# Holding the output tiles of a fused attention and gated-unit kernel back: w_out loaded late, a tile every other step, 25 tiles in a block behind the loop

## Chip, cores, metric

One core of a Trainium2 chip. The metric is device time in microseconds (us), the median of a few executions; lower is better. "Span" is the length of the one profiled execution, from which all readings of engines come. A ratio to the kernel before is of runs taken in turns on the same chip; of the experiments, a_noload, a_osb8 and a_bias_odd shared a session with the changed kernel (after_again), the others are compared with it across sessions. A run more than 1.5% above the fastest of its kernel is called slow; fast runs are compared with fast ones.

## The reference, cut to what matters

```python
# q, k, v: [8 batches, 8 heads, 576, 64]
scores = scale * q @ k.T                                   # heads 0-3: sliding window of 32 keys ("plain")
                                                           # heads 4-7: 32 keys, every 4th ("dilated")
x   = softmax(where(mask, scores, -1e9)) @ v               # -> x: [8, 576, 512]
gate = sigmoid(causal_conv(x, conv_w))                     # 5 taps, per channel
out = (gate * (x @ w_val)) @ w_out                         # [8, 576, 512], w_*: [512, 512]
```

## The kernel before

32 steps, one for each pair of heads: four steps a batch, the first two plain, the last two dilated. A step computes scores, exponential, mask and attention product of its pair, normalizes it (xn), and convolves an earlier pair (in the loop, the last but one). A batch that is complete puts eight value products (`vals`) in a list. Their results `y` put output tiles (`outs`, 128 rows x 512 columns, four 512-column products and one eviction each, that is ScalarE's copy of the result out of PSUM, the memory that TensorE writes) in another, and the steps take from both lists. Steps 0 to 7 follow a hand-written program; I call them and what precedes them the **head**, steps 8 or 9 to 31 the **loop**, what follows the start of the first convolution behind the loop (that of pair 30) the **end**.

```python
    def trans_rest(g):                  # last 64 rows of q and k: two transposes, then VectorE's copies
        ...
            nc.vector.tensor_copy(t["kT"][:, :, RM:S], ...)
            for z in range(2):
                nc.vector.tensor_copy(t["qT"][:, z, :, TM:T], ...)
    def make_bias_d():                  # mask of the dilated pairs: GpSimd, and one VectorE minimum
        ...
            nc.gpsimd.affine_select(out=mb, ...)
        nc.vector.tensor_tensor(out=mb, in0=mb, in1=same..., op=ALU.min)
    program = [ "J J T A J J", ... "C M N X V V A T O", "C M N X O K A Q R J J" ]   # O: output tile, J: filler
    ...
    setup_conv_w()
    make_conv_diag(0)
    make_conv_diag(1)
    ...
    next_pair(-1)                       # transposes of pair 0, the rest included
    for i in range(NP):
        ...                             # loads of later groups
        if i == 0:
            make_bias_d()
            prep_v(0)                   # v of pair 0 to bf16, on GpSimd: one cast
        ...
        scores(i, 0); scores(i, 1)
        if i < EARLY: early_rest(i); continue
        if i == ACT_V: upper_v(i)       # ACT_V = 8: two v casts on ScalarE
        run_conv(i - 1); apply_mask(i, 0); after_x(i - 1)
        ...                             # transposes of the next group
        apply_mask(i, 1)
        if c == 0 and outs: run_out()
        elif vals: run_val()
        attn_v(i, 0); attn_v(i, 1); normalize(i)
        ...
        for _ in range((2 if len(outs) > 2 else 1) - (c == 0 and i > NCH)):
            if outs: run_out()
        if vals: run_val()
    ...                                 # two convolutions, 8 value products, 8 tiles
```

The softmax here doesn't subtract the row's maximum and nothing guards it: scores larger than these inputs give would overflow.

## Time and profile before

| | before |
|---|---|
| median of the first three runs | 179.99 us |
| span | 178.5 us |
| first product of step 9's convolution | 56.07 us |
| ... of the first convolution behind the loop | 160.44 us |
| tiles in steps 0 to 7, 8 to 31, behind the loop | 2, 26, 8 |

I use the starts of the convolutions as marks: one a step, all on TensorE. They cut the span into head (56.07), loop (104.37) and end (18.06); step 8's tile lies ahead of the first mark, so by the marks the tiles are 3, 25 and 8. For brevity "the last convolution" below is that first one behind the loop.

### The profile page before, as it was taken

What the parts mean: (1) busy time and instruction counts of PE and PEld (TensorE: products, weight loads), DVE (VectorE), ACT (ScalarE), POOL (GpSimd) and SP (SyncE); (2) the same over time, 40 slices, a digit from 0 to 9 for tenths busy, and PEclk for the clock granted to TensorE, in tenths of its full rate; (3) what the DMA queues carried; (4) which work ended last, traced back from release to release, by engine and by line L of the source; (5) the groups of instructions that cost most, each with busy time, mean ns of one, the idle gap of its engine ahead of it and who ended that gap; (6) DMA issues with size and microseconds to landing.
All of it is one profiled execution on the core that took longest, in us unless ns stands there. A gap on an engine that the chain in (4) does not pass through costs nothing.

```text
span 178.5 us, 7036 instructions
## 1 busy us (share of the span) xinstructions
PE 162.0 (91%) x2925; PEld 107.6 (60%) x2925; DVE 126.0 (71%) x315; ACT 116.9 (66%) x217; POOL 95.8 (54%) x162
## 2 busy tenths in 40 slices
PE   6889888789859999999999999999999999999990
PEld 1445545556447656667766676677667766665540
DVE  5755643996767897779778877987697969773320
ACT  3256556646887776777876788677967796564441
POOL 6633457979663999976089718681998000000000
PEclk9999999999999999999999999999999999999998
DMA  4998999999999999999998999999997222224355
GB/s 150 238 260 269 302 220 231 356 344 212 276 321 252 307 338 309 214 313 305 273 214 257 313 305 254 301 320 299 278 338 223 59 62 62 61 62 109 99 164 162
DMA packets 48731, 42.09 MB, mean 236 GB/s; under 512 B 6853, under 2 KB 43061, under 8 KB 48698
## 3 DMA queue, kind: packets, MB, share of 16 engines
q1 hardware_dynamic: 48144, 41.49, 85.8%
q8 instruction: 23, 0.38, 0.9%
q10 hardware_dynamic: 554, 0.14, 0.4%
q14 instruction: 10, 0.08, 0.2%
HBM read 32.18 MB, written 9.44 MB: 233 GB/s over the span
## 4 chain that ended last, share of the span: by engine, by line
PE 71%; DMA 10%; DVE 7%; SPq 5%; ACT 3%; issue 1%; ACTq 0%
PE ps_bank L703 18%; PE ps_bank L686 15%; PE ps_bank L661 11%; PE ps_bank L408 5%; DMA q_nat<-in_q_dram 5%; PE ps_sc L566 4%; PE ps_sc L580 3%; PE ps_sc L513 3%; DMA vPst<-in_v_dram 3%; DMA qk_rest<-in_k_dram 3%; PE ps_bank L615 3%; PE ps_sc L530 3%; PE ps_bank L681 2%; SPq L128 2%; DVE xn L596 2%; PE ps_bank L628 2%
## 5 line engine op out<-in xcount | busy, mean ns | idle before, releaser
L534 ACT ACTIVATE et<-ps_sc 128x576 bf16<-128x576 f32 x64 | 38.7, 649 | 17.5 <-PE ps_sc L513 11.8
L708 ACT ACTIVATE osb<-ps_bank 128x512 f32<-128x512 f32 x36 | 21.9, 609 | 25.7 <-PE ps_bank L703 17.2
L692 DVE SCALAR_TENSOR_TENSOR y<-gate,ps_bank 128x288 bf16<-128x288 bf16 x64 | 28.4, 451 | 10.7 <-PE ps_bank L686 8.0
L661 PE MATMUL ps_bank<-xT,conv_diag 64*64 64x288 bf16 (+1 forms) x768 | 27.4, 266 | 0.3 <-DVE xn L603 0.3
L596 DVE TENSOR_TENSOR xn<-ps_sc,rec 128x768 bf16<-128x768 f32 (+1 forms) x27 | 25.8, 956 | 0.9
L670 ACT ACTIVATE gate<-ps_bank 128x288 bf16<-128x288 f32 x64 | 23.0, 420 | 3.8 <-PE ps_bank L661 3.7
L661 PEld LDWEIGHTS <-conv_diag 64*64 64x64 bf16 x768 | 18.8, 106 | 3.5 <-DVE qB L487 1.0
L703 PEld LDWEIGHTS <-y 128*128 128x128 bf16 x144 | 12.5, 97 | 13.2 <-ACT gate L670 1.6
L630 DVE COPY xT<-ps_bank 128x576 bf16<-128x576 bf16 x32 | 14.6, 455 | 8.2 <-PE ps_bank L628 4.3
L686 PE MATMUL ps_bank<-xT,w_val_b 128*128 128x288 bf16 x128 | 19.8, 286 | 0.2 <-DVE xT L630 0.2
L703 PE MATMUL ps_bank<-w_out_s,y 128*128 128x512 bf16 x72 | 18.4, 380 | 1.4 <-ACT gate L670 1.4
L703 PE MATMUL ps_bank<-w_out_b,y 128*128 128x512 bf16 x72 | 18.4, 379 | 0.0
L545 DVE TENSOR_TENSOR et<-et,mask_d 128x576 bf16<-128x576 bf16 x28 | 14.6, 525 | 5.4 <-ACT et L534 5.2
L545 DVE TENSOR_TENSOR et<-et,mask_p 128x576 bf16<-128x576 bf16 x26 | 15.4, 597 | 2.5 <-ACT et L534 2.5
L197 POOL CAST k_b<-k_nat 128x512 bf16<-128x512 f32 x10 | 6.9, 715 | 18.4 <-PE ps_bank L661 5.6
L686 PE MATMUL ps_bank<-xT,w_val_s 128*128 128x288 bf16 x96 | 15.5, 285 | 0.0
L686 PEld LDWEIGHTS <-w_val_b 128*128 128x128 bf16 x128 | 11.7, 98 | 4.3 <-DVE xn L603 0.3
L214 POOL CAST vP<-vPst 48x768 bf16<-48x768 f32 x14 | 12.4, 884 | 0.9
L213 POOL CAST vP<-vPst 32x512 bf16<-32x512 f32 x14 | 9.1, 650 | 6.8 <-DMA vPst<-in_v_dram 2.5
L219 POOL CAST vA<-v_st 128x512 bf16<-128x512 f32 x16 | 10.6, 660 | 4.0 <-DMA v_st<-in_v_dram 4.0
L595 DVE RECIPROCAL rec<-ps_sc 128x12 f32<-128x12 f32 (+1 forms) x27 | 6.2, 230 | 8.1 <-PE ps_sc L566 7.3
L686 PEld LDWEIGHTS <-w_val_s 128*128 128x128 bf16 x96 | 9.1, 97 | 4.3
(118 smaller groups left out, 314.9 us busy)
## 6 DMA issues: line engine op xcount, KB each, us to landing
k_nat<-in_k_dram SPq DMA_DIRECT2D x12, 512.0 KB, 5.9
q_nat<-in_q_dram SPq DMA_DIRECT2D x12, 512.0 KB, 7.5
vPst<-in_v_dram SPq DMA_DIRECT2D x6, 576.0 KB, 8.1
v_st<-in_v_dram SPq DMA_DIRECT2D x6, 512.0 KB, 6.5
k_nat<-in_k_dram SPq DMA_DIRECT2D x8, 256.0 KB, 4.8
q_nat<-in_q_dram SPq DMA_DIRECT2D x8, 256.0 KB, 6.2
out_dram<-osb SPq DMA_DIRECT2D x8, 256.0 KB, 6.3
out_dram<-osb SPq DMA_DIRECT2D x8, 224.0 KB, 5.0
```

Source lines behind the costliest of these rows:

```text
L214: nc.gpsimd.tensor_copy(x[0:48], w[0:48])
L219: nc.gpsimd.tensor_copy(vAs[b % NVD][:, a:e, :, 0:D], t["vst"][:, a:e, :].rearrange("p h (r d) -> p h r d", r=DIL))
L534: nc.scalar.activation(out=e3, in_=ps[:, :, 0:HB], func=AF.Exp, scale=scale)
L545: nc.vector.tensor_tensor(out=e3, in0=e3, in1=m, op=ALU.mult)
L596: nc.vector.tensor_tensor(out=dst, in0=av[:, :, :, 0:D], in1=rec[0:R, :, :, None].to_broadcast([R, 2, 6, D]), op=ALU.mult)
L630: nc.vector.tensor_copy(xTs[b % NXT][:, c, :, 2:], pr)
L661: nc.tensor.matmul(out=pss[G][D * hp:D * hp + D, o * T:(o + n) * T], lhsT=conv_diag[D * h:D * h + D, c, K - 1 - m, :], rhs=xt[D * h:D * h ...
L670: nc.scalar.activation(out=gate, in_=pss[G][:, 0:HB], func=AF.Tanh, scale=0.5)
L686: nc.tensor.matmul(out=ps[:, 0:HB], lhsT=w[:, mc, c * 128:(c + 1) * 128], rhs=xt[:, mc, 2 * G:2 * G + 2, 2:], start=(mc == 0), stop=(mc == ...
L692: nc.vector.scalar_tensor_tensor(out=y_half[G][:, c, b % YB * HB:(b % YB + 1) * HB], in0=gates.pop((b, c, G)), scalar=1.0, in1=ps[:, 0:HB] ...
L703: nc.tensor.matmul(out=ps, lhsT=y_half[G][:, c, y0:y0 + 128], rhs=w[:, c, :], start=(c == 0), stop=(c == NCH - 1),)
L708: nc.scalar.mul(out=osb, in_=ps, mul=0.5)
```

## The change

Its intent: keep the products of all batches on chip (`y` for eight batches instead of four), load w_out two steps later and cast and swap it only in steps 8 to 12, make one output tile in every other step, and the other 25 densely behind the loop. To make room, one weight staging buffer goes, v's staging shrinks to 96 partitions, and the first batch's v goes the way of the others (three casts on GpSimd and one on ScalarE instead of one); the buffers of xT go from 3 to 2 and those of the gate from 16 to 12. Some of the start is reordered with it; among other things the rest transposes of pair 0 leave `next_pair(-1)` and come behind `scores(0, 0)`.

```diff
-    YB = 4
+    YB = 8
-    w_st = [consts.tile([128, NCH, Dm], FP32, name=f"w_st{i}") for i in range(2)]
+    w_st = consts.tile([128, NCH, Dm], FP32, name="w_st")
-    ACT_V = 8
+    ACT_V = (0, 1)
...
-        "C M N X V V A T O",
-        "C M N X O K A Q R J J",
+        "C M N X V V A T",
+        "C M N X K A Q R J",
...
-    setup_conv_w()
-    make_conv_diag(0)
-    make_conv_diag(1)
-    warm(2)
-    next_pair(-1)
+    warm(8)
+    next_pair(-1, ("k", "q"))
...
         if i == 0:
+            prep_v(0)
             make_bias_d()
-            prep_v(0)
...
+            if i == 8:
+                cast_out()
+            elif 8 < i < 13:
+                for h in range(2):
+                    swap_out(h, i - 9)
...
         scores(i, 0)
+        if i == 0:
+            trans_rest(0)
+            setup_conv_w()
         scores(i, 1)
...
-        if c == 0 and outs:
-            run_out()
-        elif vals:
+        if c > 0 and vals:
             run_val()
...
-        for _ in range((2 if len(outs) > 2 else 1) - (c == 0 and i > NCH)):
-            if outs:
-                run_out()
+        if c % 2 == 0 and i >= 10:
+            run_out()
```

## The prediction

> **What bounds the kernel now.** I read the page first, then the chain that ended last, then waits of TensorE, then the timeline of single steps. On the page I want to know which engine is full, and when. The digits are tenths of busy time in 40 slices of 4.46 us:
>
> ```profile
> span 178.5 us, 7036 instructions
> ...
> PE   6889888789859999999999999999999999999990
> ...
> DVE  5755643996767897779778877987697969773320
> ...
> PEclk9999999999999999999999999999999999999998
> DMA  4998999999999999999998999999997222224355
> ...
> PE 71%; DMA 10%; DVE 7%; SPq 5%; ACT 3%; issue 1%; ACTq 0%
> ```
>
> TensorE is full from about 55 us, its clock is granted throughout, and the DMA engines look full until 137 us. The last line, the chain, says who matters: TensorE carries 71%, DMA 10%. Followed in order of time, the chain's last DMA piece is a q load that lands at 29.7 us; afterwards it holds compute alone. So the full DMA row costs nothing after 30 us. The waits of TensorE between 55 and 160 us sum to 1.1 us. That invites the conclusion that every product taken out of the loop shortens it. One step (pair 30) says otherwise; columns are start, duration, engine, line, what, and in brackets the wait before:
>
> ```profile
> 152.31 0.27 PE L530 MATMUL ps_sc<-qA,kA 64*128 64x128 bf16 x4
> ...
> 152.53 0.81 PE L661 MATMUL ps_bank<-xT,conv_diag 64*64 64x288 bf16 x24
> ...
> 153.75 0.46 DVE L630 COPY xT<-ps_bank 128x576 bf16<-128x576 bf16 x1
> ...
> 154.12 0.45 DVE L545 TENSOR_TENSOR et<-et,mask_d 128x576 bf16<-128x576 bf16 x1
> ...
> 154.62 0.30 PE L580 MATMUL ps_sc<-vA,et 128*128 128x65 bf16 x4 [0.24 <-DVE et L545]
> ...
> 154.83 1.02 PE L703 MATMUL ps_bank<-w_out_b,y 128*128 128x512 bf16 x4
> ...
> 155.30 0.96 DVE L596 TENSOR_TENSOR xn<-ps_sc,rec 128x768 bf16<-128x768 f32 x1
> ...
> 156.43 0.27 PE L530 MATMUL ps_sc<-qA,kA 64*128 64x128 bf16 x4
> ```
>
> This is a ring. The second half of the scores is written to the same PSUM tile in each step, and the attention product writes over it; so scores of the next step need the normalization (xn) of this one. Scores at 152.31, mask done at 154.57, attention product done at about 154.99, reciprocal, xn done at 156.26, next scores at 156.43. Without any other work the ring takes 156.30 - 152.31 = **4.0 us**. The output tile at 154.83 lies inside the wait for xn: it fills time that the ring spends anyway. TensorE and the ring are nearly level, and the wait list shows only whichever comes last.
>
> The end of the kernel is dense output tiles:
>
> ```profile
> 171.08 2.90 PE L703 MATMUL ps_bank<-w_out_s,y 128*128 128x512 bf16 x12
> ...
> 173.20 0.60 ACT L708 ACTIVATE osb<-ps_bank 128x512 f32<-128x512 f32 x1 [0.27 <-PE ps_bank L703]
> 174.07 0.60 ACT L708 ACTIVATE osb<-ps_bank 128x512 f32<-128x512 f32 x1 [0.27 <-PE ps_bank L703]
> ...
> out_dram<-osb SPq DMA_DIRECT2D x2, 256.0 KB, 2.6
> ```
>
> The evictions are 0.87 us apart: four 512-column products a tile. ScalarE needs 0.60 and waits 0.27 each time. The last line (DMA issues after 160 us) gives 2.6 us from issue to landing for a whole tile.
>
> **What the Trainium skill says.** "TensorE: Matmul & The Clock Gate", Back-to-back issue gap, gives N/2.4 + 2.5 ns for one matmul at full clock: 216 ns for 512 columns, 0.86 us a tile. The trace's 0.87 agrees; the 379 ns in the table of groups is a modelled end, not a rate. "Perfetto Trace Analysis", Identifying the Most-Contended Engine, says that matmul busy time does not measure how near TensorE is to its limit; the ring above is this case's instance. "DMA: Bandwidth & Descriptors", Anatomy of one DMA, puts a fixed 2.0 us or so on a transfer, most of it the receipt of the write (fitted there on the GpSimd path; here SyncE issues). The trace's 2.6 for 256 KB agrees roughly. "SBUF — State Buffer", Who interferes with whom, says that a VectorE operation with two SBUF inputs blocks against GpSimd operations that read SBUF. The trace agrees: the same mask multiplication takes 0.45 us alone and 0.89 at 94.7 us beside a GpSimd cast.
>
> **The change, part by part.** I follow the order of instructions that both programs issue.
>
> *Count of tiles.* There are 36 output tiles. Before: 2 in steps 6 and 7, 26 in steps 8 to 31, 8 after the loop. After: none, 11 (every even step from 10), and 25. So 17 tiles move behind the loop.
>
> *Added at the end.* 17 tiles x 0.87 = 14.8 us on TensorE, with nothing left to overlap. 9 of the 25 lie between value products; 16 are dense. For these I ask whether the four output buffers keep up: eviction 0.60, hand-over 0.1, first of usually two issues 0.4, landing 2.6: 3.7 us, over four buffers 0.93 us a tile. 256 KB in 0.87 us is also 301 GB/s, and the busiest slice of the page before shows 356. I estimate 1.0 us a dense tile: 16 x 0.13, some 1.6 to 2 us more. ScalarE (0.60) and issuing (1.8 issues x 0.42 = 0.75) stay below. Sum of the end: **+16.4 us**.
>
> *Saved in the loop, steps 9 to 31.* Taken from conv start to conv start, by place in the batch:
> - Second pair (six steps, mean 4.58 us): loses one tile, but its ring (scores, mask, 0.55 attention product, 0.95 xn) gives about 4.2: -0.4 each, -2.3.
> - Third pair (six steps): had 1, 1, 2, 2, 1, 1 tiles and keeps one each: two tiles, -1.7.
> - Fourth pair (six steps): 4.2 us, ring 4.0, so -0.2 each; the last has no successor and gains a whole tile: -1.9.
> - First pair (five steps, mean 4.62): its tile moves from ahead of the attention product to behind the normalization. Ahead of it, it filled the wait for the mask (products of the transposes end 89.92, mask ends 90.34); now TensorE waits about 0.4: +0.35 each, +1.7.
> - Batch 2 gets its swapped value products in halves: four times (0.61 - 0.49): +0.5.
>
> Sum **-3.7 us**, against 15 tiles x 0.87 = 13.0 that a bare count of TensorE time would give.
>
> *Saved ahead of the loop.* The first v loads bring 96 partitions instead of 128: 2 x 98 KB less at about 260 GB/s, 0.7 us on the chain to 29.7 us. Their extra casts (three on GpSimd, one on ScalarE, about 2.3 us for one) delay steps 0 and 1 by about a microsecond, which step 3's wait for k takes up. In step 7 the chain runs over a tile's eviction (45.69) ahead of the kT copy (46.29): without it, -0.95. In step 8 two ScalarE casts of 0.83 hold up the gate, and TensorE waits 1.4 us at 53.06; they go, together with the tile there: about -1.9. Sum **-3.6 us**. w_out itself is loaded later, but no chain waited on DMA then, so this is worth nothing.
>
> *Total.* 178.5 + 16.4 - 3.7 - 3.6 = 187.6 us of span; the timed median is 1.5 above the span: **189 us**.
>
> **The rivals.** (1) *TensorE is the loop's limit*, as the busy row says. Then all 13.0 us come back in the loop and, with 3.6 ahead of it, the kernel ends at about 180 us: same. For it speaks that TensorE is at 5.00 of 5 us in most windows; against it the 0.24 us wait in step 30 despite a tile there, and VectorE at 14.3 to 15.8 us per batch of 17.7 to 19.0, which leaves little. (2) *The writes bound the dense end*: with a landing of 4.6 us, the median over the whole run, four buffers give 1.35 us a tile, 6 us more than I have: 195 us. Against it: 2.6 us at the end, when no loads run. (3) *The loop was slowed by DMA contention of loads and stores*; with stores held back it would run faster, to perhaps 175 us. Against it: the waits of TensorE in the loop contain no DMA, and loads end 23 us ahead of the loop. (4) *GpSimd falls behind in steps 8 to 12*, where casting and swapping w_out now lie ahead of v's casts (2.4 + 5.2 us); that would cost 1 to 3 us. In steps 9 to 13 it is already 17.9 of 19.0 us busy; still, it worked a step ahead.
>
> **Range and chances.** The end is the safest term (+14.8 to +20), the loop the least safe (-1 to -9), the head -1.5 to -4.5. I take 185 to 193 us. Over 183.6 is slower by 2%; for less the loop would have to give back twice what I have: slower 0.92, same 0.06, faster 0.02.
>
> **What would show it.** In the profile after: 16 tiles at the end with evictions about 1.0 us apart, ScalarE waiting there on a landed output DMA rather than on TensorE; steps without a tile near 4.0 to 4.2 us, with TensorE idle ahead of scores waiting on xn, and ahead of the attention product of each first pair waiting on the mask; the loop's end only 6 to 9 us earlier than 160.4; no 1.4 us wait in step 8. Wrong it would be if steps without a tile take 3.7 us or less (the ring is not the limit), or if dense evictions are over 1.2 us apart.

## More of the kernel before

How the loop and the end are read is in the prediction. One place that it did not look at matters later, so here it is: GpSimd (POOL) and VectorE (DVE) near 8 us in the timeline of the kernel before; columns are start, duration, engine, line, what, and the idle time before it with its releaser.

```profile
7.11 0.50 POOL L339 TENSOR_SCALAR_AFFINE_SELECT bias_d<-bias_d 128x32 bf16<-128x32 bf16 x2
8.12 0.35 DVE L478 COPY qT<-ps_bank 128x64 bf16<-128x64 bf16 x2
8.78 0.81 DVE L342 TENSOR_TENSOR bias_d<-bias_d,same 128x32 bf16<-128x32 bf16 x1
```

GpSimd builds bias_d while v is still on its way (its cast of v begins at 8.62); the copies that the scores of pair 0 need stand ahead of VectorE's minimum, and that minimum waits for nobody.

## The result, and the profile after

The changed kernel is correct and takes **202.14 us** (199.83, 202.63, 203.56, 201.65; the third is slow); the kernel before took 180.54 us on the same chip. The ratio is 1.115, 95% interval 1.1028 to 1.1271: slower, as predicted, but 9 us above the upper end of the predicted range. A second session gave 200.21 us and a ratio of 1.111. A ratio here is the mean time of one kernel's fast runs over that of the other's in the same rounds, so it is not quite the ratio of the medians. The profiled run is the fastest of the four, 199.83 us, so the readings below explain 10.5 us of the miss and not the 13 between the medians.

The page of the changed kernel, the rows that answer to those shown of before (a slice is now 4.95 us):

```profile
span 198.1 us, 7099 instructions
...
PE   6557889677788999888789798988989899999950
...
PEclk9955999999999999999999999999999999999995
DMA  5999999999978997899399868992021022456885
...
PE 56%; DVE 16%; DMA 10%; ACT 5%; SPq 4%; issue 4%; POOL 2%; ACTq 0%; POOLq 0%
```

TensorE has fallen from 9 to 8 or 7 in many slices of the loop, and VectorE's share of the chain has risen from 7 to 16%. Two things are new at the start: slices 2 and 3 of TensorE hold 5, and its clock was granted at half in slices 3 and 4. By the marks:

| part | predicted | measured | difference to before |
|---|---|---|---|
| head, to step 9's convolution | 52.5 | 59.60 | **+3.5** instead of -3.6 |
| loop | 100.7 | 103.16 | **-1.2** instead of -3.7 |
| end | 34.5 | 35.34 | +17.3 instead of +16.4 |
| span | 187.6 | 198.1 | +19.6 instead of +9.1 |

(The predicted column is before's value plus the prediction's term.) Of the 10.5 us that the span lies above the prediction, 7.1 are in the head, 2.5 in the loop, 0.9 in the end.

**The head.** The timeline of the changed kernel at the place shown above:

```profile
7.25 0.61 POOL L199 CAST vP<-vPst 32x512 bf16<-32x512 f32 x1 [1.65 <-DMA vPst<-in_v_dram]
...
11.09 0.50 POOL L323 TENSOR_SCALAR_AFFINE_SELECT bias_d<-bias_d 128x32 bf16<-128x32 bf16 x2
11.63 0.19 DVE L326 TENSOR_TENSOR bias_d<-bias_d,same 128x32 bf16<-128x32 bf16 x1 [4.33 <-POOL bias_d L323]
...
11.94 0.34 DVE L462 COPY qT<-ps_bank 128x64 bf16<-128x64 bf16 x2
...
12.20 0.29 PE L497 MATMUL ps_sc<-qT,kT 64*64 64x96 bf16 x2 [3.42 <-DVE qT L462]
...
16.13 0.84 PE L550 MATMUL ps_bank<-vP,et 64*128 64x65 bf16 x23 [1.43 <-ACT vP L215]
```

Read it backwards. TensorE waits 3.42 us for a copy into qT whose transpose had ended near 8 us. The copy is late because VectorE stands at the minimum on bias_d for 4.33 us; the minimum waits for GpSimd, which first had to wait for v to land and make three casts of it, until 9.6 us. The Trainium skill, "TensorE: Matmul & The Clock Gate", section "Architectural detail: the array is 16× 32×32, not 1× 128×128", says of the queues that VectorE's and ScalarE's are strictly first in, first out; the trace agrees, the first of the copies starts at 11.73, 0.1 us after the minimum began. Then comes ScalarE's cast of v, for which the first attention product waits another 1.43 us. One more piece of the +3.5 us is neither: TensorE stands still for 1.42 us at 39.6 us with no engine to wait for ("issue", see below). The second trace of this kernel has 0.16 us there and reaches step 9 at 58.37 us, 2.3 us later than the kernel before.

**The loop.** The waits of TensorE between step 9 and the last convolution (59 to 163 us); columns are total, times, longest:

```profile
PE ps_sc L514 <- DVE xn L580: 3.0, 6, 0.5
PE ps_sc L497 <- DVE xn L580: 2.6, 5, 0.6
PE ps_sc L550 <- DVE et L529: 1.8, 5, 0.6
PE ps_bank L606 <- issue: 0.9, 1, 0.9
...
```

With the smaller ones cut here (one of them for a DMA, a v load, 0.6 us), 1.1 us of waiting became 9.8 us. Eleven times the next scores wait for xn and eight times the attention product waits for the mask (et), as the prediction's ring has it. New, and not in the prediction, is "issue": TensorE stood still with no engine to wait for.

**The end.** ScalarE's evictions in the dense block:

```profile
179.55 0.60 ACT L692 ACTIVATE osb<-ps_bank 128x512 f32<-128x512 f32 x1 [0.27 <-PE ps_bank L687]
180.83 0.60 ACT L692 ACTIVATE osb<-ps_bank 128x512 f32<-128x512 f32 x1 [0.69 <-DMA out_dram<-osb]
182.77 1.22 ACT L692 ACTIVATE osb<-ps_bank 128x512 f32<-128x512 f32 x2 [1.34 <-DMA out_dram<-osb]
```

The first follow TensorE at 0.87 us; then ScalarE waits for a landed write, and over the whole block of 16 the mean spacing is 1.08 us (1.13 in the second trace).

### The profile page after: what moved, and what is told of

Same layout as the page of the kernel before. It is cut to its first block, busy times and chain, and to the rows that moved or that the text cites. A ratio compares the mean times of both kernels' runs of the same rounds, so it can differ in the third digit from the quotient of the medians.

```text
span 198.1 us, 7099 instructions
## 1 busy us (share of the span) xinstructions
PE 165.3 (83%) x2939; PEld 109.9 (55%) x2939; DVE 124.6 (63%) x313; ACT 120.6 (61%) x217; POOL 99.0 (50%) x168
## 4 chain that ended last, share of the span: by engine, by line
PE 56%; DVE 16%; DMA 10%; ACT 5%; SPq 4%; issue 4%; POOL 2%; ACTq 0%; POOLq 0%
PE ps_bank L645 10%; PE ps_bank L670 10%; PE ps_bank L687 8%; DVE xn L580 6%; DMA out_dram<-osb 5%; PE ps_bank L392 4%; PE ps_sc L497 3%; PE ps_bank L599 3%; PE ps_sc L550 3%; DMA v_st<-in_v_dram 3%; DMA vPst<-in_v_dram 3%; DVE et L529 3%; PE ps_sc L514 3%; DVE xT L614 2%; SPq L698 2%
## 5 line engine op out<-in xcount | busy, mean ns | idle before, releaser
L518 ACT ACTIVATE et<-ps_sc 128x576 bf16<-128x576 f32 x64 | 39.9, 649 | 29.7 <-PE ps_sc L497 18.2
L645 PE MATMUL ps_bank<-xT,conv_diag 64*64 64x288 bf16 (+1 forms) x768 | 26.1, 265 | 0.3 <-DVE xn L587 0.3
L670 PE MATMUL ps_bank<-xT,w_val_b 128*128 128x288 bf16 x128 | 20.8, 286 | 1.8 <-issue 1.4
L687 PEld LDWEIGHTS <-y 128*128 128x128 bf16 x144 | 13.7, 98 | 13.9 <-issue 1.3
L199 POOL CAST vP<-vPst 32x512 bf16<-32x512 f32 x16 | 10.1, 632 | 17.1 <-PE ps_bank L670 7.6
L200 POOL CAST vP<-vPst 48x768 bf16<-48x768 f32 x16 | 13.8, 863 | 1.0
L201 POOL CAST vP<-vPst 32x768 bf16<-32x768 f32 x16 | 13.7, 856 | 1.0
L497 PE MATMUL ps_sc<-qT,kE 64*64 64x96 bf16 x192 | 9.5, 213 | 5.5 <-DVE xn L580 2.6
L670 PE MATMUL ps_bank<-xT,w_val_s 128*128 128x288 bf16 x80 | 13.1, 286 | 0.0
L497 PE MATMUL ps_sc<-qT,kT 64*64 64x96 bf16 x192 | 9.6, 213 | 3.6 <-DVE qT L462 3.6
```

Source lines behind the costliest of these rows:

```text
L200: nc.gpsimd.tensor_copy(x[0:48], w[0:48])
L497: nc.tensor.matmul(out=ps[D * z:D * z + D, sl, 96 * n:96 * n + 96], lhsT=kk[p0:p0 + D], rhs=t["qT"][p0:p0 + D, a // 2, :, 24 * m:24 * m + 24],
L518: nc.scalar.activation(out=e3, in_=ps[:, :, 0:HB], func=AF.Exp, scale=scale)
L645: nc.tensor.matmul(out=pss[G][D * hp:D * hp + D, o * T:(o + n) * T], lhsT=conv_diag[D * h:D * h + D, c, K - 1 - m, :], rhs=xt[D * h:D * h ...
L670: nc.tensor.matmul(out=ps[:, 0:HB], lhsT=w[:, mc, c * 128:(c + 1) * 128], rhs=xt[:, mc, 2 * G:2 * G + 2, 2:], start=(mc == 0), stop=(mc == ...
L687: nc.tensor.matmul(out=ps, lhsT=y_half[G][:, c, y0:y0 + 128], rhs=w[:, c, :], start=(c == 0), stop=(c == NCH - 1),)
```

## The experiments

Sixteen runs were made, two of them repeats. My theory after reading: (H) the head is lost to VectorE standing behind GpSimd; (L) the loop is a ring, and 0.5 to 2 us more were lost to TensorE's own instructions arriving late; (E) the end is bound by the writes in one of three ways. Rivals are named at each.

### Head: which reordering costs it

**a_bias_first** puts GpSimd's order back:

```diff
-            prep_v(0)
             make_bias_d()
+            prep_v(0)
```

> The changed kernel with one swap undone: on GpSimd the mask of the dilated pairs (bias_d) is built ahead of the v casts of pair 0, as in the kernel before. Theory (in-order chain): in the changed kernel v's casts end at 9.6 us, bias_d at 11.6, VectorE's minimum on bias_d stands ahead of the kT/qT copies, TensorE stalls 3.4 us at 12.2 us and its clock is granted at half for the next slices. With the swap undone the 3.4 us stall goes, the clock row of the page shows 9 in slices 2 to 4, the convolution of step 9 starts 3 to 6 us earlier than 59.84 us (54 to 57), and the kernel takes 4 to 7 us less than the changed one, 194 to 198 us. Rival (the three casts instead of one and ScalarE's share of them cost the time by themselves): at most 2 us are saved, 199 us or more, and the attention product of pair 0 still waits for ScalarE's cast.

Measured: 195.24 us (ratio to before 1.0874), step 9 at 54.58 us, **5.0 us earlier** than in the first trace of the changed kernel and 3.8 earlier than in the second; without their issue waits it is 3.6 against either. The 3.42 us wait is gone, and VectorE's minimum comes 4.1 us sooner:

```profile
7.49 0.19 DVE L326 TENSOR_TENSOR bias_d<-bias_d,same 128x32 bf16<-128x32 bf16 x1 [0.24 <-POOL bias_d L323]
```

The rival (the additional casts cost it) is refuted for the large part: they are all still there, and a wait of 1.37 us for ScalarE's cast too. One of my expectations was wrong: the clock row still dips (0.50 from 9 to 14 us). A repeat, **a_bias_first_2**, shows no dip, and step 9 came no earlier (55.05 us); its time was 194.92 us.

> The run with bias_d first once more, unchanged, as the control of the run without w_out's swaps in the same session. It should take 193.5 to 196.5 us again; the loop from step 9's convolution to the last one 101.5 to 103.5 us, issue waits 0 to 2 us at other places than before.

So the half clock was not what cost the head. It was also absent in a run below with the changed kernel's own head (a_noload), which reached step 9 at 60.28 us.

**b_bias_late** makes the same swap alone in the kernel before.

> The kernel before with only that swap done: v casts of pair 0 ahead of bias_d on GpSimd. Theory: VectorE's minimum moves from 8.8 us to about 11 us (one cast instead of three, so a little earlier than the 11.6 of the changed kernel), TensorE stalls 2 to 3 us there, the clock drops for some 10 us, and the kernel takes 2 to 5 us more than before, 182 to 185 us, with the convolution of step 9 later by the same amount (58 to 61 instead of 56.2). Rival (order on GpSimd is harmless, step 3's wait for k takes it up): within 1 us of before.

Measured: 182.24 us, ratio 1.0152 (1.0076 to 1.0228), step 9 at 57.57 us, 1.5 us later. The size in time is as expected, but the 2 to 3 us stall of TensorE is **not** there, nor does the clock drop. That the size fits is luck: pair 0's convolution is only 0.1 us later (21.88 against 21.77), and the rest comes in at 26.5 us, where TensorE waits 1.39 us for a q load to land (0.34 us before, at 25.05). Whether the swap delayed that load is not shown. Here VectorE's minimum stood waiting too, 2.57 us, but behind the copies that TensorE needed:

```profile
7.83 0.34 DVE L478 COPY qT<-ps_bank 128x64 bf16<-128x64 bf16 x2
...
11.15 0.19 DVE L342 TENSOR_TENSOR bias_d<-bias_d,same 128x32 bf16<-128x32 bf16 x1 [2.57 <-POOL bias_d L339]
```

So the swap alone is not the whole cause. The change made a second move: it issues the rest transposes behind scores(0, 0), hence behind the minimum. **a_rest_early** takes only that move back:

```diff
-    next_pair(-1, ("k", "q"))
+    next_pair(-1)
...
-            trans_rest(0)
             setup_conv_w()
```

> The changed kernel with the other of the two moves undone: the rest transposes of pair 0 (and with them VectorE's copies into kT and qT) are issued ahead of the scores again, so they stand ahead of VectorE's minimum on bias_d; bias_d itself stays behind v's casts on GpSimd. In the kernel before, that order of GpSimd alone gave no stall of TensorE but 1.5 us at step 9. Theory (it takes both moves: the copies that TensorE waits for stand behind a minimum that waits for GpSimd): the 3.4 us wait at 12 us goes; the minimum at about 11.5 us now holds up only VectorE's kE copy of pair 1; step 9's convolution starts 2.5 to 4.5 us earlier than the changed kernel's 58.4 to 59.6, 54.5 to 57 us, and the time is 195.5 to 199 us. Rival (bias_d's lateness by itself is the cause): less than 1.5 us earlier, 199 us or more.

Measured: 196.71 us (ratio 1.0918), step 9 at 55.79 us, **3.8 us earlier** than in the first trace and 2.6 earlier than in the second, with bias_d as late as ever (minimum at 12.02 us). TensorE now waits 2.39 us at the first attention product, for VectorE's copy of the convolution's weights, which still stands behind that minimum; that I had not expected. Undoing either move takes away most of the loss: it is the two together, a VectorE instruction that waits for GpSimd, and the copies that TensorE needs put behind it.

**a_head_b** takes the whole start of the kernel before (v of batch 0 in 128 partitions and one cast, no ScalarE casts, the early set-up and order), with the held-back tiles.

> The changed kernel with the whole start of the kernel before (v of batch 0 in 128 partitions and one cast, no ScalarE casts of v, bias_d first, the convolution's set-up and the rest transposes early, the early program's fillers as before); outputs held back, w_out late and the tile order at the end as in the changed kernel. Theory: the miss of the prediction lies in the start alone, so this lands where its terms for the end (+16.4) and the loop (-1.2 measured, -3.7 predicted) and the tile and casts gone from steps 7 and 8 (-2.9) put it: 188 to 192 us, step 9's convolution at 53 to 55 us. Rival (loading, casting and swapping w_out late disturbs steps 8 to 16 and costs the rest): 194 us or more with step 9 at 54 to 56 us, the loop longer than 104 us, and the stalls of steps 15 and 16 still there.

Measured: 194.35 us (ratio 1.0842), above the expected range. Step 9 is where it should be, at 53.73 us, 2.3 us earlier than before; the loop is not, 104.84 us. By these figures the rival (w_out's late work disturbs the loop) did as well as the theory; a_nosw below takes up its GpSimd part. The longest of TensorE's issue waits in it:

```profile
PE ps_sc L565 <- issue: 1.0, 1, 1.0
```

With three more of 0.41 to 0.45 us, at 55.9, 70.2 and 105.4 us, these make 2.3 us; without them the loop would take 102.5 us, as the others do. The rest of the head is small: all that is left of the new start in a_bias_first, the additional casts among it, costs at most about a microsecond (54.58 and 55.05 against 53.73, but a_nosw, with the start of a_bias_first, reaches step 9 at 53.57).

### Loop: the ring, the late instructions, GpSimd

**a_all36** makes no tile in the loop at all (the two lines that call `run_out` in the loop are removed).

> The changed kernel with no output tile in the loop at all: all 36 behind it, 27 of them dense. Ring theory (a step takes 4.1 to 4.3 us by scores, exponential, mask, attention product, normalization, whether or not a tile fills its waits): the loop gives back little for the 11 tiles taken out, 1 to 5 us; the end grows by 11 x (0.87 to 1.08) = 9.6 to 11.9; total 5 to 10 us above the changed kernel, 205 to 212 us. Rival (TensorE's work sets the step): the loop gives back 11 x 0.87 = 9.6 us, steps fall to 3.5 us, and the total stays within 2 us of the changed kernel.

Measured: 208.91 us (ratio 1.1639), loop 99.98 us: 11 tiles, 9.6 us of TensorE time, gave back 3.2. The end grew by 11.6. That is the ring theory's number, and the waits are the ring's:

```profile
PE ps_sc L514 <- DVE xn L580: 5.6, 12, 0.6
PE ps_sc L497 <- DVE xn L580: 2.6, 5, 0.6
```

The fastest steps take 3.98 to 4.05 us, the 4.0 us of the prediction. But a tile is not free everywhere. In the clean steps 24 and 28 (first pairs) it costs 4.79 - 3.98 = 0.81 us, nearly all of it, in steps 26 and 30 (third pairs) 0.22 and 0.11. So "TensorE is the limit" and "the ring is the limit" both hold, by turns, within one batch.

**a_bias_odd** takes VectorE's mask out of the odd steps, which carry no tile, and lets TensorE add it to the scores instead.

> The changed kernel with VectorE's mask multiplications (two of 0.45 to 0.9 us) taken out of the odd steps from 9 on; there TensorE adds the mask to the scores by four products with the identity, as in steps 0 to 4 (+0.49 us of TensorE time). Odd steps carry no output tile. Theory (ring: scores, exponential, mask, attention product, normalization): the mask's 0.45 to 0.7 us leave the ring and the products of the first half lie beside the exponential, so odd steps get shorter or stay, by 0 to 0.4 us each, in spite of more TensorE work. Rival (TensorE is the limit): each odd step gets 0.49 us longer, the loop by 5 to 6 us, 205 us or more.

Measured: 206.11 us (ratio 1.1357, two of the four runs slow). The two fast runs, 204.05 and 204.96 us, are 4.4 us above those of the changed kernel in the same session, and the loop is 4.6 us longer than there (108.24 against 103.64): near the rival's number. The trace shows that the experiment was badly aimed: the mask products come ahead of the odd step's scores, so they land in the interval that ends there, which is the one with the tile. There TensorE is the limit (xn is done at 154.69 us, TensorE gets to the mask product at 155.33):

```profile
153.74 0.95 DVE L580 TENSOR_TENSOR xn<-ps_sc,rec 96x768 bf16<-96x768 f32 x1
...
155.33 0.41 PE L485 MATMUL ps_sc<-bias_p,ident 128*128 128x288 bf16 x2
```

Those intervals grew from 4.79 to 5.52 us, while the odd ones behind them hardly moved (4.31 to 4.18 in the second pair, 4.02 to 4.09 in the fourth), although their masks were gone: the fourth pair still waited 0.64 us for xn. It tells the intervals apart; it does not tell what the mask alone is worth. I take no more from it.

**Late instructions.** The two issue waits in the changed kernel's trace, and what the DMA queues moved in the 0.1 us from 36.9 us:

```profile
39.62 0.65 PE L670 MATMUL ps_bank<-xT,w_val_b 128*128 128x288 bf16 x4 [1.42 <-issue]
88.58 0.22 PE L606 MATMUL ps_bank<-perm,xn 96*128 96x96 bf16 x1 [0.90 <-issue]
```

```profile
q8 instruction: 1, 0.02, 83.8%
```

Queue q8 moves 23 packets and 0.38 MB in a run, 16.5 KB each. The Trainium skill, "Runtime: NRT & Kernel Launch", section "Instruction fetch mechanics", says that an engine's instructions come in blocks of 16 KiB, 256 instructions, by a DMA queue of its own, and that the cost is "mostly hidden". TensorE has 2939 + 2939 matmuls and weight loads, 23.0 such blocks: the packets are its instructions, by count. I located the packet ahead of nine issue waits in four traces (the changed kernel, a_bias_first, a_head_b, a_all36): TensorE went on 2.5 to 3.1 us after the packet began, in all nine. In the trace of before, packets come as often and no wait follows.

**after_again** and **a_noload** test that. The first is the changed kernel once more. The second loads nothing for batches 4 to 7 (a wrong result):

```diff
     def load_group(g):
+        if g >= 8:
+            t = grp_tiles[4 + g % 4]
+            grp_tiles[g] = {n: x for n, x in t.items() if n in ("k", "q", "rest", "vst", "vBst")}
+            return
```

> The changed kernel once more, unchanged, for a second trace. What is asked: do the waits of TensorE that the profile calls 'issue' (no engine waited for; 1.42 us at 39.6 and 0.90 us at 88.6 us in the first trace) come back, and where. Theory (TensorE's own instructions arrive late: each such wait ended 2.5 to 3.1 us after one packet of the queue named 'instruction' began): some come back, 1 to 3 us in sum, not at the same places, each again 2.5 to 3.1 us after such a packet. Rival (a fixed hazard of the program): the same places, the same lengths. The 3.4 us wait at 12 us and the half clock come back in either case. Time 200 to 203 us.

> The changed kernel without loads of q, k and v for batches 4 to 7 (they compute on the data of batches 2 and 3, so the result is wrong on purpose); all else is as in the changed kernel. From about 65 us on the DMA engines carry only the 11 output tiles and TensorE's instructions. Theory (the late instructions come from full DMA engines): no issue wait over 0.3 us after 70 us, and the loop is shorter than in the changed kernel by its issue waits there, 1 to 2 us; the ring's steps keep 4.1 to 4.3 us. Rival 3 of the prediction (DMA contention slows the loop itself): steps fall below 4.0 us and the loop by over 4 us. Third reading (TensorE fetches too late whatever the DMA engines do): issue waits stay at 0.5 to 2 us. The end does not change (35 us).

after_again: 200.21 us, the wait at 12 us again (3.65), the half clock again, step 9 at 58.37; one issue wait of note, 0.67 us at 109.1, 2.5 us behind a packet. Of the first trace's two, the one at 88.6 did not come back, the one at 39.6 shrank to 0.16. The kept traces say more, if one counts TensorE's weight loads and matmuls together in order of start. All 18 traces hold 31 issue waits over 0.15 us after the first 10 us; 29 of them come 174 to 189 instructions past a multiple of 256, and each of the 29 ends 2.4 to 3.1 us after a packet began. One place, instruction 951 or 952, has a wait in six of the seven traces that share the changed kernel's head (1.42, 0.16, 1.15, 0.40, 2.00, 0.49 us); another, 3502, has 0.56 to 0.75 us in five. So the **places** are fixed by the program, one in every block of 256, as late instructions want it; whether a place stalls, and how long, differs between executions. a_noload: 200.74 us, the DMA row falls to 0 to 2 tenths from 59 us on, and between 64 and 163 us there is **no** issue wait, only the ring and smaller ones:

```profile
PE ps_sc L518 <- DVE xn L584: 3.0, 6, 0.5
PE ps_sc L501 <- DVE xn L584: 2.6, 5, 0.6
PE ps_sc L554 <- DVE et L533: 1.5, 6, 0.5
PE ps_sc L568 <- DVE et L533: 0.7, 3, 0.3
PE ps_bank L396 <- DVE y L680: 0.3, 1, 0.3
```

The xn waits equal those of the changed kernel to the tenth, and the loop takes 102.36 us, 0.8 and 1.3 us less than in the two traces with loads. That refutes the prediction's rival 3 (contention slows the loop itself, by many microseconds). It fits late instructions under full DMA engines, but one trace without loads is not proof: a_osb8_qg below had no issue wait in its loop either and took 102.35 us, with loads.

**a_nosw**, a_bias_first without GpSimd's eight swap copies of w_out (wrong), asks whether w_out's work, moved under the loop, slows the masks. Between 58 and 94 us the mean mask multiplication takes 0.66 us in after_again against 0.52 before. The skill's "SBUF — State Buffer", Who interferes with whom, named in the prediction, gives a mechanism. The premise is weak, though: it is 0.54 in the first trace of the changed kernel, and 0.67 in b_bias_late, whose loop is that of the kernel before.

> The run with bias_d first, and GpSimd's eight swap copies of w_out (4.9 us of its time in steps 9 to 12) taken out; one fill with zeros in step 5 stands in, so tiles of the swapped half are wrong on purpose. Theory (w_out's work moved under the ring: GpSimd is busy without a gap from 55 to 99 us, and the mask multiplications, which [...]lie on the ring, take 0.55 to 0.7 us on average instead of 0.47): GpSimd catches up about 5 us earlier, the mean mask between 58 and 94 us falls towards 0.5 us, the loop gets 0.5 to 2 us shorter than 102.4 us. Rival (the masks have room, the loop's smaller gain comes from the ring and the late instructions alone): loop within 0.4 us, apart from issue waits.

Measured: 195.04 us, with two of four runs slow; loop 102.98 us against 103.84 in its control. Without the issue waits that is 102.2 against 101.7. The mean mask did not fall either (10.16 us for 16, against 8.93 for 14). **My theory fell**: taking 4.9 us of GpSimd's copies out changed nothing in the loop that I can measure. (Its two fast runs, 194.49 and 192.4 us, lie lower than the control's, but so does its step 9, by 1.5 us.)

### End: what binds a dense tile

**a_osb8** gives the dense block eight output buffers (every other late tile is evicted into w_st, which is free by then). **a_osb8_qg** also issues those tiles' writes from GpSimd (the two lines with `eng`; without them all go through SyncE).

```diff
+        osb_n[0] += 1
+        eng = nc.sync
+        if osb_n[0] > 20 and osb_n[0] % 2:
+            osb = w_st[:, (osb_n[0] // 2) % NCH, :]
+            eng = nc.gpsimd
+        else:
             osb = out_pool.tile([128, Dm], FP32, name="osb")
```

> The changed kernel with eight instead of four output buffers in the dense end: from the 21st tile on, every other tile is evicted into slices of w_st, which is free by then. Theory (four buffers bind the dense end: an eviction each 1.08 us, ScalarE waiting on an output DMA): evictions 0.87 us apart, bound by TensorE, and the end shorter by up to 16 x 0.2 = 3 us, 197 to 200 us. Rival (the rate of the writes binds: 256 KB in 1.08 us is 243 GB/s): evictions run ahead at 0.87 for some tiles, then the last landing comes no earlier, and the time is within 1 us of the changed kernel; or the number of writes in flight binds (at most eight were open at once), with the same outcome and ScalarE or the issuing queue waiting at eight open writes.

> The run with eight output buffers in the dense end, and half of its tiles' writes issued from GpSimd, which is idle there, instead of all from SyncE. With eight buffers alone the evictions ran 0.87 us apart and the last began 28.0 us after the last convolution, but SyncE issued without a gap at 0.99 us a tile (1.75 issues of some 0.42 us and the waits between them), so the last write landed no earlier. Theory (the issuing queue binds the end): the end shrinks from 35.6 to 32.5 to 34 us, the time to 198 to 200 us. Rival (the DMA engines' rate, about 250 GB/s in the end, binds): the end stays at 35 us or more, with writes taking longer to land.

a_osb8: 202.20 us, end 35.6 us (35.3 and 36.3 in the two traces of the changed kernel): no gain, though its evictions now run 0.87 us apart. a_osb8_qg: 200.22 us, end 36.5 us, evictions still at TensorE's pace:

```profile
189.25 0.60 ACT L700 ACTIVATE w_st<-ps_bank 128x512 f32<-128x512 f32 x1 [0.27 <-PE ps_bank L689]
190.11 0.60 ACT L700 ACTIVATE osb<-ps_bank 128x512 f32<-128x512 f32 x1 [0.27 <-PE ps_bank L689]
```

The last eviction begins 28.0 us behind the last convolution in both, 31.2 and 32.1 in the changed kernel, and the last write lands no earlier. Neither the buffers nor the issuing queue bind. By windows of 4 us, the last three columns being clock, DMA share and GB/s, a_osb8_qg shows the DMA engines nearly full:

```profile
182.00:186.00 4.00, 4.00 (x21) 1.78 (x19) 0.00 (x0) 2.67 (x6) 2.59 (x5) 1.00 0.88 246
186.00:190.00 4.00, 4.00 (x19) 1.65 (x17) 0.00 (x0) 2.78 (x5) 1.62 (x4) 1.00 0.92 240
```

In the next 4 us the writes that are left go at 275 GB/s and 0.93. 256 KB at 243 GB/s are 1.08 us, the spacing that the changed kernel had with four buffers. What is left is the rate of the writes; no run with fewer bytes tests that directly.

### Two terms of the prediction without the rest

The prediction's two smaller terms of the head can be had without the rest of the change. **b_noactv** is the kernel before with `ACT_V = -1` (GpSimd casts all of pair 8's v); **b_noactv_o** also drops the tile from step 7's program (`O` in "C M N X O K A Q R J J").

> The kernel before with one thing of the change: ScalarE no longer casts two v pieces in step 8, GpSimd does (ahead of time). Theory (a term of the prediction: two casts of 0.83 us hold up the gate and TensorE waits 1.4 us at 53.06 us): the 1.4 us wait goes, step 9's convolution starts at 54.7 to 55.2 instead of 56.1 us, the time falls by 0.9 to 1.5 us. Rival (GpSimd, 8 of 10 us busy there, is late with the two casts, or VectorE's y takes over as the releaser): under 0.4 us.

> The same, and the output tile of step 7 taken out of the path to the kT copy (it is made later in the loop). Theory (another term of the prediction: its eviction lies on the chain to kT, 0.95 us): 0.6 to 1.0 us less than the run without this, 1.5 to 2.5 us less than the kernel before, 177 to 178.5 us; the tile comes back in a later step for 0 to 0.8 us. Rival (the place is filled by another wait, or the tile costs its whole 0.87 later): within 0.3 us of the run without this.

b_noactv: 179.13 us, ratio 0.996 (0.9902 to 1.0018). The 1.40 us wait for the gate is gone from the waits, step 9 starts at 53.77 us, 2.3 us earlier, more than expected; but the loop took 105.1 us instead of 104.4, with an issue wait of 0.87 us in it. b_noactv_o: **177.78 us, ratio 0.9875 (0.9808 to 0.9941)**, step 9 at 51.82 us, the loop 106.2 us with an issue wait of 1.18 us. It is 1.2% under the kernel before, the fastest that I found, and within the 2% that count as the same. What comes out of the head is partly given back in the loop: by the issue waits, and in b_noactv_o by the tile dropped from step 7, which is made there (26 tiles between the marks instead of 25; the interval from step 10's convolution grows from 4.60 us in b_noactv to 5.47).

**b_wval_mid** and **b_wval_late** start from b_noactv_o and load w_val's 1 MB behind the q of step 4; the second also reorders the casts and value products there.

> The kernel before without ScalarE's v casts and without the tile of step 7 (177.8 us), and w_val's 1 MB load moved behind the k and q of step 4, which were the last transfer on the chain (landed at 27.8 to 29.7 us). Theory: that q lands 3 to 4 us earlier; w_val then lands about 27 us and its four casts (2.4 us) become the limit of the first value products, so 0.5 to 2 us come out of it: 175.5 to 177.5 us. Rival (TensorE waits for the casts instead): within 0.5 us, or slower.

> The same, with the v cast of pair 4 ahead of w_val's casts on GpSimd and the two value products of step 4 behind its attention product, so that the casts have about 2 us more. Theory: 0.5 to 1.5 us below the run with the load moved alone, 174.5 to 176.5 us, over 2% under the kernel before. Rival: no gain over that run, since the late attention product hands the delay to step 5.

b_wval_mid: 182.79 us (ratio 1.014), b_wval_late 178.49 us (0.9901): no gain over b_noactv_o, and both miss their expected ranges. In the first, the attention product of step 4 waits 0.76 + 1.56 us for v casts that now stand behind w_val's on GpSimd: the in-order queue again.

## Why the prediction was wrong, point by point

- **The direction** was right; the sum was 189, measured 202.14 and 200.21.
- **End, +16.4: right**, measured +17.3 and +18.3 in the two traces of the changed kernel. The spacing of about 1.0 us was 1.08 to 1.13, but its reason was wrong, so the nearness is partly luck: the estimate took it from four buffers and a landing of 2.6 us, and the two runs with eight buffers point to the write rate. The prediction had set that aside with a slice of 356 GB/s, in which loads ran; the writes of the end reach 240 to 275.
- **Head, -3.6: wrong, and the larger part of the miss.** The step that failed is "Their extra casts (three on GpSimd, one on ScalarE, about 2.3 us for one) delay steps 0 and 1 by about a microsecond, which step 3's wait for k takes up." It counted the casts and not what else stands behind them in two in-order queues. In its place the runs show a wait of 3.42 us (3.65 in the second trace) of TensorE for copies that stand behind VectorE's minimum on bias_d, which stands behind GpSimd's casts. To step 9, GpSimd's order undone alone gives 3.8 to 5.0 us, the place of the rest transposes alone 2.6 to 3.8; the larger figures are against the first trace and hold its issue wait of 1.42 us, which the prediction did not have either. The casts themselves cost a microsecond at most by step 9. With the old start the head is at -2.3; the two terms of steps 7 and 8, predicted at -0.95 and -1.9, measured -2.0 and -2.3 at step 9 in the kernel before; the 0.7 us for smaller v loads was not tested alone. That a delay of the start is taken up was half right. In a_bias_first, with all the casts, pair 0's convolution is 2.7 us later than before and pair 4's only 0.4 (39.25 against 38.83); what the two queues added was not taken up, 3.8 us at pair 0's (28.25 against 24.44) and still 3.6 at step 9, issue wait aside.
- **Loop, -3.7: the mechanism right, the size off.** It measured -1.2, -0.7, -2.0 and -0.5 in the two traces each of the changed kernel and of a_bias_first; without the issue waits -1.4 to -2.9. The kernel before has one trace, and b_bias_late and b_noactv, with the same tiles in the loop, took 105.3 and 105.1 us instead of 104.4, so a microsecond of this is scatter. By place in the batch (a_bias_first against before): second pairs -1.1 instead of -2.3, third -1.3 instead of -1.7, fourth -1.0 instead of -1.9, first +1.3 instead of +1.7; batch 2's halves, +0.5, lie somewhere in these. So the terms that failed are the floors: second pairs run at 4.3 to 4.7 us and not at 4.2, fourth pairs at 4.0 to 4.4 and not at 4.0. A sum was off too: the six second pairs of the kernel before average 4.69 us by these marks, not 4.58.
- **Rival 1** (TensorE is the limit) fails as the story of the whole loop (a_all36: 3.2 of 9.6 us come back), but holds for first pairs, where a tile costs 0.81 us. **Rival 2** (writes bind the end) was right in kind and wrong in size: 1.08 us a tile, not 1.35 (its own terms give 5.7 / 4 = 1.43). **Rival 3** is refuted by a_noload (by "ahead of the loop" the prediction means the loop's end: loads stop near 137 us). **Rival 4** (GpSimd falls behind): GpSimd is busy without a gap longer than before, but a_nosw shows no cost in the loop.
- **Left open**: why TensorE's instructions come late in some executions and not in others (the trace of before shows no such wait, nor do four of the sixteen in the loop; none in any trace comes after 111.3 us, though loads go on to about 135 us in all but a_noload), and what the smaller counts of xT and gate buffers do, though no long wait of TensorE names them.

## What to carry to other kernels

When an instruction moves on one engine, follow who waits for its result on the others, and then list what stands behind that waiter in its queue: a 0.2 us minimum cost TensorE 3.4 us. Work taken out of a loop that is a ring gives back only what the ring does not need, a third of it here, while the same work behind the loop costs all of it. Before adding buffers to a dense end, compare its bytes per tile with the DMA rate that the trace shows there.

## What the Trainium skill lacked or had wrong

- "Runtime: NRT & Kernel Launch", Instruction fetch mechanics, calls the crossing of a 16 KiB block mostly hidden. Here TensorE stood 0.16 to 2.0 us at some blocks while the DMA engines were full, up to 2.5 us in sum in one run, and went on 2.4 to 3.1 us after the block's packet began. The page gives no sign by which to see it; in this profile it is "issue" ahead of a matmul together with a packet of q8, at the same instruction count modulo 256 (174 to 189) each time.
- "TensorE: Matmul & The Clock Gate", Part 1: The HAM clock gate, ties the half clock to an idle window of about 3.4 us. a_bias_first was granted 0.50 from 9 to 14 us with no wait over 1.4 us there and its repeat, the same program, 1.00. The page's warning that the window runs free fits; its threshold alone does not foretell the dip.
- No page that I used gives a rate for writes of 128 rows of 2 KB from one core: 240 to 275 GB/s in the dense end of a_osb8_qg, at 0.88 to 0.93 of the DMA engines' time.
